# A smaller lead of the score maxima: 90 slots in place of 96 in a two-branch attention kernel

## The chip, the cores and the metric

The kernel runs on one NeuronCore of a Trainium2 chip. The metric is the device time of one execution in microseconds (us). The time before is 1738.96 us, the median of three runs (1738.92 to 1739.48). Engines are named as the profile names them: PE (TensorE matmuls) and PEld (its weight loads), DVE (VectorE), ACT (ScalarE), POOL (GpSimd), SP (SyncE, which here only starts transfers).

## What is computed

Two attention branches over the same 2048 x 512 input are mixed by a gate. A is softmax attention with 32 heads of 16 dimensions; B cuts the sequence into four segments of 512 rows, has causal softmax inside a segment, and adds a linear memory of the earlier segments.

```python
def reference(A_x, A_wqkv, A_wo, B_x, B_wq, B_wk, B_wv, B_wo, B_beta, gate_w):
    ...
        scores = jnp.einsum("bhqd,bhkd->bhqk", q, k) * scale
        p = _softmax(scores, axis=-1)
        o = jnp.einsum("bhqk,bhkd->bhqd", p, v)
    ...
        for s in range(N):
            logits = jnp.einsum("bhqd,bhkd->bhqk", qs, ks) * scale + mask
            p = _softmax(logits, axis=-1)
            a_dot = jnp.einsum("bhqk,bhkd->bhqd", p, vs)
            a_mem = num / den
            o = g * a_mem + (1.0 - g) * a_dot
    ...
    g = _sigmoid((x * gate_w).sum(-1, keepdims=True))
    return g * a + (1 - g) * b
```

## The kernel before

**Two stages.** The first stage makes queries, keys and values of both branches. It is cut into steps of 12 matmuls of 512 columns; work that goes beside them is posted on a step's number (`post_at`). From step S0 = 50 on come 32 steps for branch B's queries and keys, "segment tiles" (tile `pr`, line 385). Its memory is made beside them (tiles `tps`, `mps`, `num`, `den`).

The main stage runs over 2368 slots. A unit is four heads by one segment of 512 query rows: 32 units of A with 64 slots each (four heads by 16 blocks of 128 keys) and 32 of B with 10 slots. They alternate, an A unit and a B unit making 74 slots; at the end B comes before A. In a slot PE computes one score tile (tile `st`, line 1065; 50 rows of contraction: 48 of query and key and two that carry the row's maximum), and ACT takes its exponential into tile `p` (line 1088).

**The maxima.** A softmax row's maximum has to be known before its scores are made, since it enters the score product as two extra rows. So every score product is made once more, earlier, for its maximum alone: PE makes the product (tile `sm`, line 242), DVE reduces it (line 275 for A, line 290 with the causal mask for B). The list `maxs` holds all 2368 in the order in which they are made; slot n of the main stage makes the maximum of number n + LEAD. The first LEAD maxima are made in the first stage, in groups of four (`some_max`), beside the value pairs and beside some of the segment tiles. In a unit's 64 or 74 maxima the ten of a B unit stand at places that are multiples of three; `start` and `apart` say where, with special values for the unit numbers 1 and 31.

**From a maximum to its row.** After a unit's last maximum, POOL combines the partial maxima (`finish_max`). Then `transpose_max` turns them into rows on PE (tile `mt_ps`, line 232: one matmul per unit against the identity, into 32 rows of the bank), ACT copies them out (tile `mt`, line 235), and SP sends them into the query tile, behind which that unit's scores can start. `transpose_max` takes one or two units in one bank and with one copy. When it is called is set by a due number, counted in maxima: the end of the next A unit's maxima plus LATE_T = 9, but no later than `first[u] + LEAD - 12`, that is 12 slots ahead of the unit's first score. `run_late` looks at the end of every third slot and takes up to two units that are due. Where a call is made, no `fill` product is made in that step.

**Three slots at a time.** In the main stage PE makes the scores and maxima of three slots (a burst, in alternating row halves of the array), and then the value products that `most` allows (tile `ops`, line 155, with 17 columns of weights, in four strips of columns for four heads) or three products of other work from the list `shared` (in the same tile `ops`). Score tiles have three banks (`st`), maxima four (`sm`). The program's fp32 matmul shows as two in the trace.

**The end.** The last LEAD slots have no maximum to make. From slot `wide.start = nS - LEAD + 2` to `nS - 4` scores go into six banks, and steps are six slots long: up to 8 value pieces of 128 columns, and where these leave room, up to 11 less those of the products in `fill` (output products of an earlier block and the first closing products of the last one, into bank `sm`). What is left of the closing products is made behind the last value product.

Of the kernel before, what the change touches and what calls it, by code (L numbers as in the profile page):

```python
# [31 lines left out]

SLOTS = {"A": 64, "B": 10}
NU = 32
LEAD = 96
BURST = 3
LATER = (2, 3)
MOST = 3
# [9 lines left out]
def gated_mix(ctx, tc, x, xT, wqkv, a_wo, b_wq, b_wk, b_wv, b_wo, beta, gate_w, out):  # L48
# [52 lines left out]
    def unit(side, k):  # L101
        return side, k % NG, k // NG
# [15 lines left out]
    for k in range(NU):  # L118
        mine = {u: iter(range(32)) for u in range(2)}
        bs = [k - 1] if 0 < k < NU - 1 else [k - 1, k] if k else []  # L120
        theirs = {r: [(unit("B", b), (r, i)) for b in bs for i in range(5)] for r in range(2)}
        start, apart = (33, (3, 3)) if k == 1 else (6, (9, 3)) if k < NU - 1 else (23, (3, 3))
        at_ = [next(m for m in range(len(maxs) + start, len(maxs) + start + 6) if m % 3 == 0)]
        while len(at_) < 10 * len(bs):
            at_.append(at_[-1] + apart[len(at_) % 2])
        for m in range(len(maxs), len(maxs) + 64 + 10 * len(bs)):
            r = (m + 1) % 2
            if m in at_ and bs:
                maxs.append(theirs[r].pop(0))
            else:  # L130
                maxs.append((unit("A", k), (r, next(mine[r]))))
        assert not theirs[0] and not theirs[1]
    last_max = {u: m for m, (u, _) in enumerate(maxs)}
    a_last = sorted(last_max["A", k % NG, k // NG] for k in range(NU))
    first_max = {u: m for m, (u, _) in reversed(list(enumerate(maxs)))}
    assert len(maxs) == nS and all(first[u] + LEAD - last_max[u] > 24 for u in units)

# [19 lines left out]
    def wait_early(n):  # L157

        loads_ = []
        for m in range(n + 1 + LEAD, n + 1 + BURST + LEAD):  # L160
            if m < nS:
# [47 lines left out]
    def finish_max(u):  # L209
        nm = pmt.pop(u)  # L210
        if u[0] == "A":
            pm, nm = nm, mp.tile([128, 4, 4], F32, tag="nm", name="nm")
            dm = mp.tile([128, 4, 4, 2], F32, tag="dm", name="dm")
            nc.gpsimd.tensor_sub(dm, pm[:, :, :, 2:4], pm[:, :, :, 0:2])  # L214
            nc.gpsimd.tensor_scalar_min(dm, dm, 0.0)
            nc.gpsimd.tensor_add(dm, dm, pm[:, :, :, 0:2])
            nc.gpsimd.tensor_sub(nm, dm[:, :, :, 1], dm[:, :, :, 0])
            nc.gpsimd.tensor_scalar_min(nm, nm, 0.0)
            nc.gpsimd.tensor_add(nm, nm, dm[:, :, :, 0])

        ms = mp.tile([128, 2, 2, 2, 4], F32R, tag="ms", name="ms")
        nv = nm.rearrange("p (r h) s -> p r h s", r=2)
        nc.gpsimd.tensor_copy(ms[:, :, 0], nv)  # L223
        nc.gpsimd.tensor_sub(ms[:, :, 1], nv, ms[:, :, 0].bitcast(F32))
        return ms
# [37 lines left out]
    def max_part(m, bank, b=None):  # L263

        u, (r, i) = maxs[m]
        side, g, c = u
        if u not in pmt:
            pmt[u] = mp.tile([128, 4, 4] + [4] * (side == "A"), F32, tag="pm" + side, name="pm")
        pm = pmt[u]
        ps = bank()  # L270
        if side == "A":

            kc, s, h = i // 8, i % 8 // 2, 2 * r + i % 2
            max_product(ps, u, h, s, 0, CH, kt_[u, kc])
            nc.vector.tensor_reduce(pm[:, h, s, kc:kc + 1], ps, axis=AX.X, op=ALU.max, negate=True)  # L275
            was_read(b)
            flush_rows()
        else:


            k = kt_[u, c]
            if b is not None:
                read_last[b] = 9 * nS
            mine = [(2 * r + h, s, 128 * (s == 2) + 256 * (s == 1 and h), 128 * (s + 1))
                    for h, s in (((0, 0), (0, 2)), ((0, 1), (1, 1)), ((1, 0), (1, 2)), ((0, 3),), ((1, 3),))[i]]
            for h, s, n0, w in mine:
                max_product(ps, u, h, s, n0, w, k)
            flush_rows()
            def masked(h, s, n0, w):
                nc.vector.tensor_tensor_reduce(  # L290
                    out=tri["rest"][:, 0:w], in0=ps[:, n0:n0 + w], in1=tri["mask"][:, CH - w:], scale=-1.0, scalar=3.0e38,
                    op0=ALU.add, op1=ALU.min, accum_out=pm[:, h, s:s + 1])
                was_read(b)

            for h, s, n0, w in mine:
                rows_left.append(lambda h=h, s=s, n0=n0, w=w: masked(h, s, n0, w))
            rows_left.pop(0)()
        if m == last_max[u]:
            def finish():

                due = min(e for e in a_last if e >= last_max[u]) + LATE_T
                late.append((min(due, first[u] + LEAD - 12), u, finish_max(u)))
            todo.append((m + 1, finish))

    def run_todo(m):

        for e in [e for e in todo if e[0] <= m]:
            todo.remove(e)
            e[1]()

    def run_late(pool, tag, m):
        while us := [e for e in late if e[0] < m][:2]:
            for e in us:
                late.remove(e)
            transpose_max(us, pool, tag)
# [3 lines left out]
    def loads(m):  # L319

        m = min(m, len(maxs) - 1)
        while loaded[0] <= m:
            u, (r, i) = maxs[loaded[0]]
            if u not in qt:
                load_q(u)
            kc = u[2] if u[0] == "B" else i // 8
            if (u, kc) not in kt_:
                load_k(u, kc)
            loaded[0] += 1


    mnext = [0]
    with ExitStack() as p0:
# [61 lines left out]
        def post_at(n, place, f):  # L395
            posted.setdefault((n, place), []).append(f)
# [421 lines left out]
        def mem_q(c):  # L818

            banks = [me_sm.tile([128, CH], F32, tag="sm", name="num") for _ in range(4)]  # L820
            for o in range(NO):
                for i in range(4):
                    nc.tensor.matmul(banks[i][32 * o:32 * o + 32], mbd[o // 2][32 * i:32 * i + 32, o % 2].rearrange("p h e -> p (h e)"),  # L823
                                     pqs[o][32 * i:32 * i + 32], start=True, stop=True, tile_position=(32 * i, 32 * o))
            dps = me_ps.tile([128, CH], F32, tag="me", name="den")
            for o in range(NO):
                nc.tensor.matmul(dps[32 * o:32 * o + 32], zbd[:, o], pqs[o], start=True, stop=True,  # L827
                                 tile_position=(0, 32 * o))
            pqs.clear()

            ams = unit4(7, F32)

            def keep(i):
                nc.scalar.copy(ams[i], banks[i])  # L834
                nc.sync.dma_start(numd[c][i], ams[i])

            def keep_den():
                dn = wk1.tile([128, CH], F32, tag="dn", name="dn")
                nc.scalar.activation(dn, dps, AF.Identity, bias=eps)
                for o in range(NO):  # L840
                    nc.sync.dma_start(dend[c][8 * o:8 * o + 8], dn[32 * o:32 * o + 8])
            for i in range(4):
                keep(i)
            post(1, 2, keep_den)
# [35 lines left out]
        def some_max():  # L880
            m = mnext[0]
            if m == LEAD:
                return
            loads(m + 3 + PRE)
            for i in range(4):
                max_part(m + i, lambda: me_sm.tile([128, CH], F32, tag="sm", name="sm"))
            run_todo(m + 3)
            mnext[0] += 4
            run_late(me_ps, "me", mnext[0])

        post_at(36, 1, lambda: loads(16))
        for n in range(37, S0):
            post_at(n, 3, some_max)
# [6 lines left out]
        for n in range(32):  # L900
            if n in (14, 21, 29):
                post_at(S0 + n, 3, lambda c=n // 8: mem_q(c))
            elif n in (2, 4, 6, 8, 10, 12, 16, 18, 22, 24, 26):
                post_at(S0 + n, 3, some_max)

        def gates():
# [133 lines left out]

    wide = range(nS - LEAD + 2, nS - 4)
    assert wide.start % (2 * BURST) == wide.stop % (2 * BURST) == 0
# [115 lines left out]
    def octet(side, o, c, t0, vector=False):  # L1158
# [67 lines left out]
        if t0 is not None:  # L1226

            t0 += max([e + 2 - LEAD - t0 - ts[1] for e in a_last if 0 <= e + 1 - LEAD - t0 - ts[1] < 12], default=0)
        for n, f in zip(ts, (load, factors, send, factor, scale, store)):
# [117 lines left out]
    n = 0  # L1347
    while n < nS or queue or beside or filled[0] < len(fill):
# [4 lines left out]
        m = n + LEAD  # L1353
# [81 lines left out]
```

## Time and profile before

| | before |
|---|---|
| median of 3 runs | 1738.96 us |
| the profiled execution's own time | 1738.98 us |
| its span | 1737.1 us |
| first stage, up to the first score | 272.7 us |
| main stage with maxima (last DVE reduction ends) | to 1661.4 us |
| slots without maxima (last value product starts its end) | to 1715.2 us |
| closing products and the output | to 1737.1 us |

The span is the stretch between the first and the last instruction of the profiled execution; 1.9 us of its own time lie outside it. A row of a timeline gives the start in us, the time of the merged instructions, the engine, the line, the operation with tiles and shapes, and how many. Instructions on one engine can overlap in such rows, so the step from one row's start to the next one's tells more than a row's time. A row of the chain of waits gives start, time, engine and line of what released the next piece, followed back from the last instruction of the window.

### The profile page before, as it was taken

To read this page: it belongs to the slowest core of one execution; us is meant where nothing else is said; L and a number is where in the kernel's file an instruction comes from. 1 tells how busy PE (TensorE), PEld (TensorE's weight loads), DVE (VectorE), ACT (ScalarE), POOL (GpSimd) and SP (SyncE) were. 2 spreads that over 40 slices of the span, in tenths; PEclk is the share of its full clock that TensorE was granted. 3 is DMA by queue.
4 is the path that set the end of the run, shared out by engine and by line. 5 is a ranking of instruction groups with operands and counts; after the bars stand their busy time and mean duration, and the time that the engine had idled before them with its cause. 6 is when DMAs were issued, how large, how long until landed. Compare 5 with 4: busy or idle time off the path is not lost.

```text
span 1737.1 us, 41522 instructions
## 1 busy us (share of the span) xinstructions
PE 1729.1 (100%) x15157; PEld 875.5 (50%) x15157; DVE 1608.8 (93%) x3376; ACT 1439.9 (83%) x2774; POOL 706.8 (41%) x964
## 2 busy tenths in 40 slices
PE   9999999999999999999999999999999999999998
PEld 7877775444444444444444444444444444444444
DVE  7777987999999999999999999999999999999931
ACT  6543667888888888888888888888888888888884
POOL 1022544233353437444535353435354353435442
PEclk9999999999999999999999999999999999999999
DMA  7679887435453446454444453445444444444542
GB/s 246 193 241 238 303 278 218 112 93 156 116 159 102 142 124 175 132 141 125 137 138 143 133 148 122 134 140 139 141 123 149 131 141 113 144 119 147 149 152 63
DMA packets 168651, 264.97 MB, mean 153 GB/s; under 512 B 39512, under 2 KB 80760, under 8 KB 168448
## 3 DMA queue, kind: packets, MB, share of 16 engines
q1 hardware_dynamic: 166720, 260.78, 50.5%
q8 instruction: 121, 1.98, 0.5%
q0 software_dynamic: 1440, 1.14, 0.3%
q14 instruction: 82, 0.67, 0.1%
q10 hardware_dynamic: 288, 0.39, 0.1%
HBM read 177.74 MB, written 83.25 MB: 150 GB/s over the span
## 4 chain that ended last, share of the span: by engine, by line
PE 97%; DVE 1%; DMA 1%; ACT 0%; SPq 0%; issue 0%; ACTq 0%; DVEq 0%
PE ops L155 40%; PE st L1065 28%; PE sm L242 14%; PE pr L385 9%; PE pair L385 2%; PE sm L155 2%; DMA u<-xT 0%; PE mt_ps L232 0%; PE tps L851 0%; PE sm L1065 0%; DVE pm L275 0%; DMA u<-x 0%; PE mps L865 0%; PE num L823 0%; PE den L827 0%
## 5 line engine op out<-in xcount | busy, mean ns | idle before, releaser
L1088 ACT ACTIVATE p<-st 128x512 f32<-128x512 f32 x2261 | 1190.7, 600 | 146.8 <-PE sm L242 93.3
L275 DVE TENSOR_REDUCE pm<-sm 128x1 f32<-128x512 f32 x2048 | 1276.2, 682 | 8.3 <-PE sm L242 7.6
L242 PE MATMUL sm<-kA,qA 48*128 48x512 f32 x2048 | 662.2, 424 | 0.0
L1065 PE MATMUL st<-qA,kA 50*128 50x512 f32 x2014 | 655.9, 431 | 0.0
L155 PE MATMUL ops<-p,vA 128*17 128x256 f32 (+3 forms) x6360 | 552.2, 445 | 0.0
L1065 PEld LDWEIGHTS st<-qA,kA 50*128 50x128 f32 x2014 | 326.9, 185 | 423.4 <-ACT p L1088 379.7
L242 PEld LDWEIGHTS sm<-kA,qA 48*128 48x128 f32 x2048 | 337.8, 185 | 11.0 <-issue 4.2
L1189 POOL TENSOR_TENSOR rcp<-rec,minus 128x32 f32<-128x32 f32 x43 | 234.8, 5461 | 75.8 <-DMA rec<-dend 71.2
L290 DVE CUSTOM_DVE_ANT_0 rest<-sm,mask 128x128 f32<-128x128 f32 (+3 forms) x512 | 246.5, 481 | 0.0
L155 PEld LDWEIGHTS ops<-p,vA 128*17 128x17 f32 x6360 | 129.1, 96 | 215.7 <-issue 184.5
L1069 POOL TENSOR_SCALAR_AFFINE_SELECT p<-p 128x512 f32<-128x512 f32 x128 | 79.6, 638 | 267.6 <-ACT p L1088 263.1
L242 PE MATMUL sm<-kB,qB 48*128 48x128 f32 (+3 forms) x512 | 166.1, 384 | 0.0
L1065 PE MATMUL st<-qB,kB 50*128 50x512 f32 (+1 forms) x495 | 105.3, 329 | 0.3 <-ACT mt L235 0.3
L385 PE MATMUL pr<-u,u 128*128 128x512 f32 x392 | 101.4, 397 | 0.0
L1065 PEld LDWEIGHTS st<-qB,kB 50*128 50x128 f32 x495 | 68.5, 186 | 62.2 <-ACT p L1088 50.4
L155 PE MATMUL ops<-p,vB 128*17 128x128 f32 (+3 forms) x1504 | 88.3, 350 | 0.0
L385 PEld LDWEIGHTS pr<-u,u 128*128 128x128 f32 x392 | 71.8, 188 | 19.0 <-ACT u L834 2.5
L242 PEld LDWEIGHTS sm<-kB,qB 48*128 48x128 f32 x512 | 79.9, 184 | 0.0
L214 POOL TENSOR_TENSOR dm<-pm 128x32 f32<-128x32 f32 x32 | 7.8, 245 | 170.9 <-DVE pm L275 170.9
L434 POOL TENSOR_SCALAR mn<-full 128x512 f32<-128x512 f32 x24 | 39.0, 1625 | 53.8 <-ACT full L428 53.7
L223 POOL CAST ms<-pm 128x16 fp32r<-128x16 f32 x32 | 6.3, 198 | 127.5 <-DVE pm L290 127.5
L1205 POOL TENSOR_TENSOR v<-v,inv 128x512 f32<-128x512 f32 x31 | 39.8, 1284 | 28.7 <-DMA inv<-rdA 21.7
(227 smaller groups left out, 1422.5 us busy)
## 6 DMA issues: line engine op xcount, KB each, us to landing
kA<-kdA SPq DMA_DIRECT2D x256, 128.0 KB
vA<-vdA SPq DMA_DIRECT2D x31, 544.0 KB
kA<-kdA SPq DMA_DIRECT2D x256, 64.0 KB
kB<-kdB SPq DMA_DIRECT2D x192, 64.0 KB
qB<-qdB SPq DMA_DIRECT2D x192, 64.0 KB
kdA<-q SPq DMA_DIRECT2D x32, 256.0 KB
qA<-qdA SPq DMA_DIRECT2D x64, 128.0 KB
qdB<-q SPq DMA_DIRECT2D x32, 256.0 KB
```

The lines of the kernel that those rows point to most:

```text
L155: behind[0] = nc.tensor.matmul(*args, **kw)
L214: nc.gpsimd.tensor_sub(dm, pm[:, :, :, 2:4], pm[:, :, :, 0:2])
L242: nc.tensor.matmul(ps[:, n0:n0 + n], rows(qt[u][:, :, s * 128:(s + 1) * 128], h, 48), rows(k[:, :, k0:k0 + n], h, 48), start=True, stop=True)
L275: nc.vector.tensor_reduce(pm[:, h, s, kc:kc + 1], ps, axis=AX.X, op=ALU.max, negate=True)
L290: nc.vector.tensor_tensor_reduce(out=tri["rest"][:, 0:w], in0=ps[:, n0:n0 + w], in1=tri["mask"][:, CH - w:], scale=-1.0, scalar=3.0e38, op ...
L385: nc.tensor.matmul(ps, l, r, start=start, stop=stop, skip_group_check=chained)
L434: nc.gpsimd.tensor_scalar_min(ph["mn"], full, 0.0)
L1065: nc.tensor.matmul(ps[:, n0:n0 + CH - q0], rows(k[:, :, b * 128:(b + 1) * 128], h, 50), rows(q[:, :, q0:], h, 50), start=True, stop=True)
L1069: nc.gpsimd.affine_select(out=x, in_=x, pattern=[[0, 4], [1, 128]], base=0, channel_multiplier=-1, compare_op=ALU.is_ge, fill=0.0)
L1088: nc.scalar.activation(p[:, h], ps, AF.Exp, scale=SCALE)
L1189: eng.tensor_tensor(r, rec, minus, op=ALU.pow)
L1205: eng.tensor_mul(k["v"], k["v"], k["inv"])
```

## The change

LEAD goes from 96 to 90. The six maxima move from the first stage to the main stage. In the segment tiles one group of four goes (groups at S0 + 10 and S0 + 12 become one at S0 + 11), and the last group, at S0 + 26, makes two. The places of the B maxima among the maxima of units 1 and 31 are put six numbers earlier. `wide.start` is worked out from LEAD, so the end without maxima is six slots shorter.

```diff
-LEAD = 96
+LEAD = 90
...
-        start, apart = (33, (3, 3)) if k == 1 else (6, (9, 3)) if k < NU - 1 else (23, (3, 3))
+        start, apart = (27, (3, 3)) if k == 1 else (6, (9, 3)) if k < NU - 1 else (17, (3, 3))
...
-            for i in range(4):
+            for i in range(min(4, LEAD - m)):
                 max_part(m + i, lambda: me_sm.tile([128, CH], F32, tag="sm", name="sm"))
-            run_todo(m + 3)
-            mnext[0] += 4
+            run_todo(min(m + 3, LEAD - 1))
+            mnext[0] = min(m + 4, LEAD)
...
-            elif n in (2, 4, 6, 8, 10, 12, 16, 18, 22, 24, 26):
+            elif n in (2, 4, 6, 8, 11, 16, 18, 22, 24, 26):
                 post_at(S0 + n, 3, some_max)
```

On PE in the first stage, behind the step S0 + 12, the group of maxima goes and so does the transposition of the first unit's rows (`+` and `-` as in the program of the change against that of before; `u` are operands of the segment tiles):

```order
 L385 MATMUL pr<-u_1810,u_1640 128x512
 L385 MATMUL pr<-u_1809,u_1640 128x512
-L242 MATMUL sm<-kA_196,qA_1644 128x512 x4
-L232 MATMUL mt_ps<-identf,ms 32x128
 L385 MATMUL pr<-u_1809,u_1641 128x512
 L385 MATMUL pr<-u_1810,u_1640 128x512
```

The steps S0 + 12 and S0 + 13 now follow each other without a break; the group stands behind S0 + 11, ahead of `mps`, and the transposition behind the group of S0 + 16.

On PE in the main stage, at the end of the first A unit's scores, before:

```order
L1065 MATMUL st<-qA_1644,kA_199 128x512
L242 MATMUL sm_3248<-kA_196,qA_4093 128x512
L155 MATMUL ops<-p,vA 17x128 x4
L155 MATMUL ops<-p,vA 17x256 x4
L232 MATMUL mt_ps<-identf,ms 32x128 x2
L1065 MATMUL st<-qA_1644,kA_199 128x512
L242 MATMUL sm_3245<-kB_200,qB_4158 128x128
```

And now, in the same place:

```order
L155 MATMUL ops<-p,vA 17x256 x8
L232 MATMUL mt_ps<-identf,ms 32x128
L1065 MATMUL st<-qA_1644,kA_199 128x512
L242 MATMUL sm_3230<-kB_200,qB_4192 128x128
L242 MATMUL sm_3230<-kB_200,qB_4192 128x384
L1065 MATMUL st<-qA_1644,kA_199 128x512
L242 MATMUL sm_3227<-kA_196,qA_4126 128x512
L1065 MATMUL st<-qA_1644,kA_199 128x512
L242 MATMUL sm_3228<-kA_196,qA_4126 128x512
L155 MATMUL ops<-p,vA 17x256 x4
L155 MATMUL ops<-p,vA 17x128 x4
L232 MATMUL mt_ps<-identf,ms 32x128
```

A B unit and an A unit were transposed in one call. Their due numbers fall apart now: B's is `first[u] + LEAD - 12`, which came down by six, A's is nine behind the end of its maxima, which didn't. In the whole program the calls go from 33 (31 with two units) to 64 with one each, and ACT's copies (line 235) with them; 30 of the 31 calls that are added stand in the main stage with maxima, one behind it.

On PE at the end, the last closing products ahead of the last score and the first behind the last values, before:

```order
L155 MATMUL sm_3246<-wB,qclosed 128x512 x3
L155 MATMUL sm_3247<-wB,qclosed 128x512
L1065 MATMUL st<-qA_22283,kA_199 128x512
L155 MATMUL ops<-p,vA 17x512 x8
L155 MATMUL sm_3247<-wB,qclosed 128x512 x2
L155 MATMUL sm_3248<-wB,qclosed 128x512 x3
```

And now:

```order
L155 MATMUL sm_3227<-wB,kA_194 128x512 x3
L155 MATMUL sm_3227<-wA,kA_195 128x512
L1065 MATMUL st<-qA_22403,kA_199 128x512
L155 MATMUL ops<-p,vA 17x512 x8
L155 MATMUL sm_3227<-wA,kA_195 128x512 x2
L155 MATMUL sm_3228<-wB,qclosed 128x512 x3
```

The list `fill` is six products further behind: 56 in place of 50 closing products stand between the last values and the last two pairs of blocks (`hl`).

## The prediction

> **What bounds the kernel now.** I read the totals of the page first, then the chain of waits and the busy times of the main stage alone, then timelines of single bursts. All sums are made against the profiled execution's own 1738.98 us (its span of 1737.1 and 1.9 around it), which is 0.02 us above the median of the runs, 1738.96.
>
> ```profile
> PE 1729.1 (100%) x15157; PEld 875.5 (50%) x15157; DVE 1608.8 (93%) x3376; ACT 1439.9 (83%) x2774; POOL 706.8 (41%) x964
> ```
>
> PE's 100% says little, since the ends of matmuls are modelled. Two answers for the main stage say more: the busy times from 280 to 1655 us (PE, weight loads, DVE, ACT, POOL), and the chain of waits over the same stretch.
>
> ```profile
> 280.00:1655.00 1375.00, 1375.00 (x12921) 627.90 (x12921) 1374.34 (x2949) 1225.62 (x2372) 595.71 (x816) 1.00 0.47 135
> by line: PE ops L155 49.1%; PE st L1065 34.2%; PE sm L242 16.2%; PE mt_ps L232 0.4%; issue 0.0%
> ```
>
> DVE is busy for 1374.34 of 1375 us, so it is nearly full. Yet the chain runs through PE alone: not one step of it is a DVE, ACT or DMA step. Both are loaded to the brim, and the chain says whose delay counts. Two DVE rows, each an unbroken run of reductions of A maxima, tell which of the two waits (the page's row for these reductions stands ahead of them):
>
> ```profile
> L275 DVE TENSOR_REDUCE pm<-sm 128x1 f32<-128x512 f32 x2048 | 1276.2, 682 | 8.3 <-PE sm L242 7.6
> ...
> 381.29 13.83 DVE L275 TENSOR_REDUCE pm<-sm 128x1 f32<-128x512 f32 x23
> 562.45 8.81 DVE L275 TENSOR_REDUCE pm<-sm 128x1 f32<-128x512 f32 x14
> ```
>
> One reduction takes 0.68 us by itself, and they overlap. From start to start it is (13.83 - 0.68) / 22 = 0.598 us in the first run, DVE's own pace, and (8.81 - 0.68) / 13 = 0.625 in the second, slower, in gaps too short to be listed as idle time. In the second stretch DVE waits for PE, in the first it doesn't. So PE sets the pace in part of the time and DVE is just behind it in the rest; there is next to no cover for new work on PE.
>
> **Six maxima leave the first stage.** The chain there, in the segment tiles, with what follows each group:
>
> ```profile
> 193.26 0.66 PE sm L242 x4
> 193.92 0.59 PE tps L851 x4
> 194.51 2.73 PE pr L385 x12
> 197.24 0.70 PE mps L865 x59
> 197.94 2.94 PE pr L385 x12
> 200.88 0.66 PE sm L242 x4
> 201.54 0.34 PE mt_ps L232 x2
> 201.88 5.68 PE pr L385 x24
> ...
> 254.66 0.67 PE sm L242 x4
> ```
>
> All of it is PE work on the chain. The group at 193.26 goes: -0.66. It comes back ahead of `mps` at 197.24: +0.66. The group at 200.88 goes with its transposition, and so does the break in the stream of products (12 products take 2.94 ahead of a break that stands alone, 2.73 without): -0.66 - 0.34 - 0.21 = -1.21. The transposition comes back later: +0.34. The last group, at 254.66, makes two of four: -0.3, about half. Sum **-1.2 us**. DVE has six reductions fewer in this stage and is not on this part of the chain. Bounds: -0.5, if a transfer or DVE takes over somewhere, and -3.6, six reductions at 0.598, if DVE did set the pace.
>
> **Six slots of the main stage get a maximum.** DVE's full pace prices them at 6 x 0.598 = **+3.6 us**; two bursts of three slots. Value pieces and scores of these six slots come along, and they are counted off the end below. Bounds: +3.3, two of the shorter bursts (1.66 us from 390.84 to 392.50 below), and +3.75 at the slower 0.625.
>
> **The transposition is taken apart.** This is the term that decides. The order shows 30 more calls in the main stage, each with a matmul on PE, a bank of `st`, an ACT copy and its transfers; the matmuls and the transfers are no more than before, the calls are. What does a call cost PE? The bursts at 391 and at 395 us each have three value pieces ahead of the next score:
>
> ```profile
> 390.84 0.50 PE L1065 MATMUL st<-qA,kA 50*128 50x512 f32 x1
> ...
> 391.73 0.84 PE L155 MATMUL ops<-p,vA 128*17 128x384 f32 x8
> 392.50 0.50 PE L1065 MATMUL st<-qA,kA 50*128 50x512 f32 x1
> ...
> 393.43 1.06 PE L155 MATMUL ops<-p,vA 128*17 128x128 f32 x16
> ...
> 395.38 0.84 PE L155 MATMUL ops<-p,vA 128*17 128x128 f32 x16
> 396.05 0.39 PE L232 MATMUL mt_ps<-identf,ms 128*32 128x128 f32 x4
> 396.36 0.50 PE L1065 MATMUL st<-qA,kA 50*128 50x512 f32 x1
> ...
> 1660.86 0.85 PE L155 MATMUL ops<-p,vA 128*17 128x256 f32 x16
> 1661.53 0.38 PE L232 MATMUL mt_ps<-identf,ms 128*32 128x128 f32 x2
> 1661.84 0.91 PE L1065 MATMUL st<-qA,kA 50*128 50x512 f32 x3
> ```
>
> From the first value product to the next score it is 0.77 us without a call, 0.98 with a call of two units and again 0.98 with a call of one unit (x2 in the trace). So a call costs 0.21 us, whatever its units; the second unit was free, beside the first. The chain of the main stage agrees: 0.4% of 1375 us for 30 calls is 0.18 us each. Taken in full, 30 x 0.21 = 6.3 us.
>
> What could hide it is PE's waiting. There is little:
>
> ```profile
> 504.49 0.50 PE L1065 MATMUL st<-qA,kA 50*128 50x512 f32 x1
> ...
> 505.53 0.84 PE L155 MATMUL ops<-p,vB 128*17 128x128 f32 x16
> ```
>
> The score and maximum part of this burst takes 1.04 us, where others take 0.93 (392.50 to 393.43) or 0.89 (390.84 to 391.73). Such a burst stands once in two of three units, some 20 times in all, and makes about 20 x 0.13 = 2.6 us in which PE was ahead of DVE. I let half of that, 1.3 us, absorb added PE work, since a delay elsewhere in the unit isn't given back there. Term: **+5.0 us**. Bounds: 0, if DVE's pace hides it all, and 30 x 0.39 = 11.7, if the matmul's whole time in its row counted. I stay near the 0.21 that the step from row to row gives twice. ACT's copies, one more a unit, lie in ACT's free time: it is busy for 1225.62 of 1375 us.
>
> **The end.** Before, the first six slots without maxima ran from 1661.84 to the row at 1665.84: 4.00 us, because eight `fill` products stood in them. These slots are gone from the end.
>
> ```profile
> 1665.84 0.73 PE L1065 MATMUL st<-qA,kA 50*128 50x512 f32 x3
> ...
> 1668.78 0.50 PE L1065 MATMUL st<-qB,kB 50*128 50x512 f32 x2
> ...
> 1673.11 0.73 PE L1065 MATMUL st<-qB,kB 50*128 50x256 f32 x5
> ...
> 1694.66 0.72 PE L1065 MATMUL st<-qA,kA 50*128 50x512 f32 x3
> ...
> 1697.60 0.72 PE L1065 MATMUL st<-qA,kA 50*128 50x512 f32 x3
> ...
> 1715.18 1.42 PE L155 MATMUL sm<-wB,qclosed 128*128 128x512 f32 x5
> ...
> 1726.94 2.92 PE L155 MATMUL sm<-wB,hl 128*128 128x512 f32 x12
> 1729.70 2.88 PE L155 MATMUL sm<-wA,hl 128*128 128x512 f32 x12
> ```
>
> But `fill` is not less. In the steps that are left, by the order, the first two (before: 2.94 us up to 1668.78 and 4.33 from there to 1673.11, where a score had to wait for ACT's copy and seven `fill` products stood) now have four value pieces and one call each, and no `fill` product. Without `fill` a step is as long as 1694.66 to 1697.60, 2.94 us; with a call's 0.21 some 3.2, so 6.4 in place of 7.27: -0.9. The next steps with `fill` have 11, 9, 9 and 7 products where there were 9, 6, 6 and 6: nine more. A closing product takes (1726.94 - 1715.18) / 50 = 0.235 us: +2.1. And six more stand behind the last values: +1.4. That piece is PE's alone:
>
> ```profile
> 1727.59 0.42 DVE L1214 TENSOR_TENSOR hl<-v,hl 128x256 fp32r<-128x256 f32 x1
> ```
>
> The last block's operand is ready at 1728.01, and PE comes to it at 1729.70, so 1.7 us of PE work would have to go before anything else became late there. The end: -4.0 - 0.9 + 2.1 + 1.4 = **-1.4 us**. Bounds: -3.5, if the nine products that stand earlier find PE free, and 0, if a row's transfer is waited for in the two short steps and they gain nothing.
>
> **The sum.** -1.2 + 3.6 + 5.0 - 1.4 = +6.0: 1738.98 + 6.0 = **1745.0 us**, 0.35% slower.
>
> **The rivals.** (1) *The calls are hidden.* If DVE sets the pace, PE's 0.21 us lie in its waits and the sum is -1.2 + 3.6 - 1.4 = +1.0: 1740.0. For it speaks DVE's 1374.34 of 1375 us; against it that no DVE step is in the chain, and 0.625 us a reduction in the second DVE row. By the Trainium skill (Perfetto Trace Analysis, Identifying the Most-Contended Engine) the busy time of matmuls is no measure of how loaded TensorE is, the busy share of its weight loads is, and VectorE's occupancy is a fair measure; by that rule PE would be loaded to 46% (627.90 of 1375) and VectorE would be the bound, which gives this rival's time; the chain of this trace speaks against it. Chance 0.18.
>
> (2) *Faster: the B maxima come to stand better.* Relative to the scores they move six slots. In a burst with a B maximum DVE is the slower one, in bursts with four value pieces PE is; where the two coincide more often, DVE's short waits go. The second DVE row loses 13 x 0.027 = 0.4 us; if each third unit has such a stretch, that is 10 x 0.4 = 4 us. Together with hidden calls: +1.0 - 4.0 = -3.0, 1736.0. It decides only if the reductions come to 0.598 us in every run. The 30 calls load PE, which this needs to be relieved; chance 0.04.
>
> (3) *The rows come late.* A unit's rows are sent six slots nearer to its scores. Before:
>
> ```profile
> 398.25 1.27 SPq L238 DMA_DIRECT2D qA<-mt x2
> ...
> 409.16 0.50 PE L1065 MATMUL st<-qA,kA 50*128 50x512 f32 x1
> ```
>
> The issue ends at 399.52, the A unit's first score (behind ten slots of B) starts at 409.16: 9.6 us; six slots less leave 6. If the SP queue is held for longer than that in each unit, PE waits perhaps 1 us 30 times: 1770. Nothing in the profile shows such a hold; chance 0.03.
>
> That the change doesn't do what it says is excluded by the order, which shows the six maxima in their new places.
>
> **How the numbers follow.** My forecast (the calls cost PE most of 0.21 us each) has a chance of 0.75, with 1742 to 1748 as its own range. The range is to hold 8 in 10: it takes in the forecast's range but for its upper edge, and most of the hidden case, **1739.5 to 1747.5**. 0.2% is 3.5 us, about what a measurement of this kernel can tell from no change: slower than 1742.4 is nearly all of the forecast and the late rows, 0.73; within it are the hidden calls, the forecast's low edge and most of the better places of B, 0.24; faster 0.03.
>
> **What would show it.** Right: 64 calls of `mt_ps`, each some 0.2 us in the chain of waits, its share from 0.4% to about 0.8% in the main stage; the stretch from the first to the last reduction of the main stage longer by more than 8 us (3.6 for the maxima, 5 for the calls), with DVE's mean per reduction up. Also a first score about 1.2 us earlier, and about 1.4 us more between the last value product and the `hl` products. Wrong: a main stage longer by 3.6 us alone (rival 1); bursts of scores that wait for a transfer (rival 3); or a first stage that saves more than 2 us, which would mean that DVE set the pace there.

## The result, and the profile after

The changed kernel takes 1756.01 us (median of four runs, 1753.37 to 1759.05) beside 1738.94 us for the kernel before (median of four): a ratio of 1.0103, with an interval of 1.009 to 1.0115. That is 17.1 us slower, where 6.0 were forecast; the direction was right, the size was not. The profiled execution of the changed kernel took 1756.53 us, with a span of 1754.8.

The page of the changed kernel, busy times and the chain of waits by engine:

```profile
PE 1738.5 (99%) x15157; PEld 881.7 (50%) x15157; DVE 1612.7 (92%) x3376; ACT 1445.3 (82%) x2805; POOL 707.2 (40%) x964
...
PE 95%; DMA 2%; DVE 1%; ACT 1%; issue 0%; POOL 0%; SPq 0%; DVEq 0%; ACTq 0%
```

The same two views as before for the main stage of the changed kernel, 280 to 1655 us: busy times, and the chain of waits by line.

```profile
280.00:1655.00 1375.00, 1371.31 (x12832) 629.49 (x12831) 1366.21 (x2915) 1221.52 (x2385) 587.14 (x807) 1.00 0.49 134
by line: PE ops L155 48.2%; PE st L1065 33.2%; PE sm L242 16.3%; PE mt_ps L232 0.8%; DMA qB<-mt 0.4%; DMA kA<-kdA 0.3%; ACT p L1088 0.2%; POOL p L1069 0.1%; issue 0.1%; POOL v L1205 0.1%; POOL v L1207 0.1%; ACT part L1279 0.0%; SPq L238 0.0
```

Two things are new. `mt_ps` has doubled to 0.8%, as forecast. And the chain, which was PE alone before, now has transfers in it: rows of maxima (`qB<-mt`) and keys (`kA<-kdA`). DVE's idle time in this window went from 0.66 to 8.79 us (1375 less its busy time): it waited along with PE.

**Where the 17.7 us of span lie.** ACT makes one exp for each of the 2368 slots, so the starts of the exps, counted from the first, give the time of every slot in both traces. Here "both early" is an experiment told below.

| stretch | forecast | changed kernel | both early |
|---|---|---|---|
| start-up, to the 49th product of `pr` and `pair` | 0 | +2.1 | -0.3 |
| from there to the first exp | -1.2 | -1.3 | -1.5 |
| slots 0 to 2274 (30 calls more) | +5.0 | **+11.4** | +5.7 |
| slots 2274 to 2280 (six maxima more, no `fill`) | -0.4 | -0.4 | -0.3 |
| slot 2280 to the last exp | +1.2 | **+5.0** | +2.9 |
| the rest | +1.4 | +0.9 | -0.5 |
| sum | +6.0 | +17.7 | +6.1 |

The first row is no effect of the change: its code is the same. In the timeline of PE, the first product behind the value pair's eviction starts at 18.15 us before (first fence) and at 20.24 in this execution of the changed kernel (second):

```profile
18.15 0.50 PE L385 MATMUL pr<-kA,qtmp 128*128 128x512 f32 x1 [0.84 <-DVE vs L550]
```

```profile
20.24 0.50 PE L385 MATMUL pr<-kA,qtmp 128*128 128x512 f32 x1 [1.81 <-DVE vs L550]
```

In the profiles of the twelve runs told below it starts at 17.5 to 18.6 us. The exps themselves, by form, with the first and the last start behind the durations, before and after:

```profile
L1088 ACT ACTIVATE p<-st x2261: 588/598/680, 273.9 to 1713.4; 128x512 f32<-128x512 f32 x189
```

```profile
L1088 ACT ACTIVATE p<-st x2264: 588/599/682, 274.7 to 1730.3; 128x512 f32<-128x512 f32 x189
```

The first exp is 0.8 us later and not 1.2 earlier; less the 2.1 of start-up that is a gain of 1.3.

**The main stage, first cause: the calls.** A stretch without any stall shows their price. This is the view by windows, ACT's work on `p` alone; 1111 exps are 1110 slots, 15 times 74. Before:

```profile
771.18:1448.48 677.30, 583.42 (x1111) 1.00 0.46 134
```

The same slots of the changed kernel:

```profile
778.22:1458.18 679.96, 584.00 (x1111) 1.00 0.48 134
```

2.66 us more in 15 pairs of units, with one call more in each: 0.18 us a call if the calls are all of it, 5.3 us for 30. This term of the forecast was right in size. The stretch holds the shift of six slots too: in `pair_soon`, a run told below that has the shift without these calls, it takes 678.24 us, so about 1.7 of the 2.66 us are shown to be the calls'.

**Second cause: operands that come late.** The remaining 6 us of the main stage stand in a few places. Over twelve slots at a time, the slots fall behind those of the kernel before by 1.7 and 1.2 us between 478 and 498 us, by 2.4 near 676, 1.1 near 1587 and 1.4 near 1631; some of it is made up elsewhere. PE's timeline near 676 us in the changed kernel (idle time ahead of a row, and what ended it, in brackets):

```profile
670.67 0.84 PE L155 MATMUL ops<-p,vA 128*17 128x128 f32 x16
671.33 0.38 PE L232 MATMUL mt_ps<-identf,ms 128*32 128x128 f32 x2
671.64 0.50 PE L1065 MATMUL st<-qA,kA 50*128 50x512 f32 x1
...
679.35 0.38 PE L155 MATMUL ops<-p,vA 128*17 128x128 f32 x2 [1.82 <-DMA qB<-mt]
```

The call of one unit is there, 0.97 us from value product to score as forecast. But PE then stands still. The last value product of a burst carries the wait for all landings that the next three slots need (`wait_early`); here it waits for B's rows, transposed at 671.33 and copied out by ACT by 672.01. What SP did in that time:

```profile
670.96 0.58 SPq L1255 DMA_DIRECT2D blk<-hdA  x1
671.59 0.47 SPq L1255 DMA_DIRECT2D blk<-hdB  x1
672.10 0.47 SPq L1018 DMA_DIRECT2D vA<-vdA  x1
672.67 2.64 SPq L177 DMA_DIRECT2D kA<-kdA  x4
675.41 1.41 SPq L238 DMA_DIRECT2D qB<-mt  x2
```

The rows (line 238) come up only at 675.41, 3.4 us after they were ready, behind loads of the output's steps, of values and of keys. The second place is earlier, at 484.77 us, where PE waits 0.87 us for keys:

```profile
484.77 0.81 PE L155 MATMUL ops<-p,vA 128*17 128x384 f32 x2 [0.87 <-DMA kA<-kdA]
```

SP there, in the changed kernel:

```profile
472.52 0.47 SPq L1198 DMA_DIRECT2D rdA<-rec  x1
476.19 0.55 SPq L1202 DMA_DIRECT2D inv<-rdA  x1
476.80 1.96 SPq L177 DMA_DIRECT2D qA<-qdA  x4
479.18 1.69 SPq L177 DMA_DIRECT2D kA<-kdA  x4
```

SP stood from 472.99 to 476.19, because `inv` reads what the store ahead of it writes. By the Trainium skill (DMA: Bandwidth & Descriptors, Anatomy of one DMA) a transfer's wait for a semaphore is spent on the engine that issues it, before it is handed on; the trace agrees, with 3.2 us in which SP issued nothing. The loads of `qA` and `kA` stood behind it. In the kernel before they went ahead of the same pair:

```profile
464.85 1.95 SPq L177 DMA_DIRECT2D qA<-qdA  x4
466.90 1.75 SPq L177 DMA_DIRECT2D kA<-kdA  x4
...
469.24 0.40 SPq L1198 DMA_DIRECT2D rdA<-rec  x1
474.65 0.55 SPq L1202 DMA_DIRECT2D inv<-rdA  x1
```

So the change moved more than maxima. Loads of queries and keys are issued PRE = 20 numbers ahead of the maxima, and the maxima are six slots nearer to the scores; the output's steps hang on the value products, which did not move. On SP's queue, loads and rows slid six slots back between steps that wait.

**The end.** PE's waits in the last steps of the changed kernel:

```profile
1674.07 0.49 PE L1065 MATMUL st<-qA,kA 50*128 50x512 f32 x1
...
1677.64 0.77 PE L1065 MATMUL st<-qA,kA 50*128 50x512 f32 x3
...
1681.36 0.45 PE L1065 MATMUL st<-qB,kB 50*128 50x384 f32 x1 [1.06 <-ACT mt L235]
...
1684.39 0.59 PE L155 MATMUL ops<-p,vA 128*17 128x512 f32 x1 [1.25 <-DMA qB<-mt]
...
1693.38 0.38 PE L155 MATMUL ops<-p,vB 128*17 128x128 f32 x2 [1.25 <-DMA qA<-mt]
```

Two bursts of three slots with maxima take 3.57 us, as forecast (+3.6). Then the rows of the last two units, now in calls of their own and six slots apart, are waited for at three places: the copy first, then B's rows, then A's. A fourth wait of the end, 0.78 us for DVE's `res` (line 1283) at 1704.01 us, isn't in the kernel before either. It comes in all twelve runs below and was not followed up.

### The profile page after: what moved, and what is told of

Same layout as the page of the kernel before. It is cut to its first block, busy times and chain, and to the rows that moved or that the text cites. A ratio compares the mean times of both kernels' runs of the same rounds, so it can differ in the third digit from the quotient of the medians.

```text
span 1754.8 us, 41627 instructions
## 1 busy us (share of the span) xinstructions
PE 1738.5 (99%) x15157; PEld 881.7 (50%) x15157; DVE 1612.7 (92%) x3376; ACT 1445.3 (82%) x2805; POOL 707.2 (40%) x964
## 4 chain that ended last, share of the span: by engine, by line
PE 95%; DMA 2%; DVE 1%; ACT 1%; issue 0%; POOL 0%; SPq 0%; DVEq 0%; ACTq 0%
PE ops L155 40%; PE st L1065 27%; PE sm L242 14%; PE pr L385 9%; PE pair L385 2%; PE sm L155 1%; PE mt_ps L232 1%; DMA u<-xT 1%; DMA qB<-mt 0%; DMA qdB<-q 0%; ACT p L1088 0%; PE tps L851 0%; DMA qA<-mt 0%; DVE pm L275 0%; PE sm L1065 0%
## 5 line engine op out<-in xcount | busy, mean ns | idle before, releaser
L275 DVE TENSOR_REDUCE pm<-sm 128x1 f32<-128x512 f32 x2048 | 1279.7, 691 | 12.9 <-PE sm L242 11.5
L242 PEld LDWEIGHTS sm<-kA,qA 48*128 48x128 f32 x2048 | 335.5, 185 | 10.5 <-issue 4.6
L1069 POOL TENSOR_SCALAR_AFFINE_SELECT p<-p 128x512 f32<-128x512 f32 x128 | 79.8, 640 | 223.4 <-ACT p L1088 218.5
```

Source lines behind the costliest of these rows:

```text
L242: nc.tensor.matmul(ps[:, n0:n0 + n], rows(qt[u][:, :, s * 128:(s + 1) * 128], h, 48), rows(k[:, :, k0:k0 + n], h, 48), start=True, stop=True)
L1069: nc.gpsimd.affine_select(out=x, in_=x, pattern=[[0, 4], [1, 128]], base=0, channel_multiplier=-1, compare_op=ALU.is_ge, fill=0.0)
```

## The experiments

Theory 1: operands come late, because loads and rows have slid on SP's queue. Theory 2: it is the calls, which are dear. Each run has its own runs of the kernel before on the same chip; the us given as a difference are between those two medians. On this scale the changed kernel stands at +17.1.

One thing has to be read with these times, the TensorE clock that was granted. In the traces of the kernel before, of the changed kernel, of `split_only` and of `both_early` it is 1.00 from 8 us on to the last 2.1 us, so the table above compares like with like. In the other traces it falls to 0.50 for a while, during a wait of PE or soon behind it. With the last 4 us of each trace left out it is at 0.50 for 3.4 us in all in `brows_early`, `mid26`, `end_rows` and `pair_soon`, 6.8 in `rows_act`, 10.2 in `factor_later`, 13.7 in `paired`, 20.5 in `lead102`, 23.9 in `pre26` and 105.9 in `rows_pool`. There a late operand can cost more than the wait that the timeline shows; `lead102` below is an example.

### The calls taken back, or added alone

`paired`:

```diff
-                late.append((min(due, first[u] + LEAD - 12), u, finish_max(u)))
+                late.append((min(due, first[u] + LEAD - (6 if first[u] < nS - 100 else 12)), u, finish_max(u)))
```

> The changed kernel, but with the bound on a B unit's rows at LEAD-6 (the last two units keep LEAD-12), so that one call transposes two units again: 34 calls in place of 64, and B's rows are sent some four slots later. Theory 1 (operands come late): a call costs only the 0.16 us by which each pair of units is longer in the changed kernel (45.04 against 44.89 us for 74 slots), so 30 calls less give 4.8 us, and the places where PE waits for landings of qB, qA and kA stay or grow: 1751 us, or more if the later B rows add waits. Theory 2 (the calls are what is dear, with what they hold up on SP's queue): nearly all of the 17 us goes, 1741 to 1743.

Measured: 1775.39 us beside 1737.21, +38.2, ratio 1.0222 (1.0208 to 1.0236). Theory 2 is out: with the 30 calls gone the kernel is 21 us slower still. Theory 1 had said "or more". Part of it is the clock, 0.50 for 6.8 us from 685.25 on at the first of these two places in PE's timeline:

```profile
687.67 0.59 PE L155 MATMUL ops<-p,vA 128*17 128x128 f32 x2 [6.18 <-DMA qB<-mt]
...
1103.38 0.38 PE L155 MATMUL ops<-p,vA 128*17 128x128 f32 x2 [1.22 <-DMA qB<-mt]
```

The second kind comes back in every third pair of units, since a call is looked for at every third slot only. B's rows, some four slots later, miss their burst even where SP is free. So in the changed kernel the calls of one unit are not the loss: with LEAD 90 they buy rows that come in time.

`split_only`, on the kernel before:

```diff
-                late.append((min(due, first[u] + LEAD - 12), u, finish_max(u)))
+                late.append((min(due, first[u] + LEAD - 18), u, finish_max(u)))
```

> The kernel before, LEAD 96, with only the bound at LEAD-18: B's rows leave four slots sooner in calls of their own (64 calls), all maxima, loads and rows else where they were. Theory 1 (operands come late because of the six slots): only the price of 30 calls, 30 x 0.16 = 4.8 us, and no matmul that waits for a landing: 1743 to 1745. Theory 2 (the calls are dear): 1750 to 1756, with PE waiting for qB or qA as in the changed kernel.

Measured: 1746.18 beside 1737.21, +9.0, ratio 1.0053 (1.004 to 1.0065). The chain of its main stage holds nothing that is late:

```profile
by line: PE ops L155 48.8%; PE st L1065 33.7%; PE sm L242 16.5%; PE mt_ps L232 0.9%; ACT p L1088 0.1%; ACT part L1279 0.0%; issue 0.0%
```

The 1110 slots in its middle:

```profile
774.11:1454.93 680.82, 583.39 (x1111) 1.00 0.46 133
```

3.52 us more than before, 0.23 a call, 7.0 for 30. Both theories missed: the run is 3 to 5 us over theory 1's +4 to +6, and has none of theory 2's late operands. The last 1.8 us lie behind slot 2274 and were not followed up.

### Rows sooner, loads sooner

`brows_early`: the same bound, LEAD - 18, in the changed kernel.

> The changed kernel (LEAD 90) with the bound at LEAD-18: B's rows leave six slots sooner, the calls stay 64. Theory 1: the waits for qB (about 2.4 us at 676, 1.4 at 1631, 0.7 each at 496 and 1587, and at the end about 1.8 for B's last unit) go, the wait for kA at 482 us stays: about 1750. Theory 2 (the calls are dear wherever they stand): 1756.

Measured: 1751.44 beside 1737.21, +14.2, ratio 1.0084 (1.007 to 1.0097), some 3 us less than the changed kernel where 6 were expected. The waits at 1587 and 1631 us are gone, those at 482, 496 and 676 stay. At 676 the rows are issued sooner, at 672.79, but PE still waits 1.5 us for their landing; what the longer burst at 496 us waits for the profile doesn't name.

`pre26`:

```diff
-PRE = 20
+PRE = 26
```

> The changed kernel with loads of q and k 26 maxima ahead in place of 20, which puts them back to the slots they had beside scores, values and the output's steps in the kernel before. Theory 1, first half (loads of q and k have slid behind steps of the output on SP's queue): the wait for kA at 482 us goes, 1.7 to 2.4 us, and some of the waits for qB behind loads of kA or qB (676, 1631): 1750 to 1754. Theory 1, other half (only the rows are late): 1754 to 1756. Theory 2 (the calls are dear): 1756.

Measured: 1769.95 beside 1737.21, +32.7, ratio 1.0191 (1.0177 to 1.0205). A miss as a whole, and yet slots 0 to 2146 are without a stall: 4.5 us over the kernel before, the price of the calls. The loss lies around them: the first exp comes at 280.9 us, 7 us later, and the slots from 2146 to 2274 take 14 us more. In the first stage PE waits 1.8 us, up to 240.27, and the granted clock is 0.50 for 3.4 us from 240.55; the rest of the 7 us was not followed up. In the later slots PE waits 6.45 us for `kB`, up to 1643.54, and the granted clock is 0.50 from 1640.0 to 1660.5. So I put the loads forward in the middle alone.

`mid26`:

```diff
-            loads(m + PRE)
+            loads(m + PRE + 6 * (n < nS - 250))
```

> The changed kernel with loads of q and k 26 maxima ahead in slots 0 to 2117 alone, 20 in the first stage and in the last 250 slots. Theory 1 in its first half (the six slots put the loads behind steps of the output on SP's queue, and the loads stand ahead of the rows): the jumps at 482 to 498 us (2.4), 676 (2.4), and those near 1587 and 1631 (2.0) go, about 7 us: 1749. Rows late by themselves: the waits for qB at 676 and 1631 us stay, only some 3 us go: 1753. Neither: 1756.

Measured: 1749.02 beside 1739.29, +9.7, ratio 1.0053 (1.0039 to 1.0067): 7.4 us less, as the first half of theory 1 has it. No key is waited for in the main stage any more, and of the waits for rows a single one is left, at 673 us.

`end_rows`:

```diff
-                late.append((min(due, first[u] + LEAD - 12), u, finish_max(u)))
+                late.append((min(due, first[u] + LEAD - 12) - 6 * (first[u] > nS - 80), u, finish_max(u)))
```

> The changed kernel with the rows of the last two units one group of six slots sooner. If the end is longer because these rows come late (PE waits there for ACT's copy of the transposed rows, for qB and for qA, 0.8 + 1.75 + 1.75 us beyond the usual step): 3.5 to 4.3 us less, about 1752. If it is longer because closing products that had found PE free now stand in its way: no change, 1756.

Measured: 1753.32 beside 1739.29, +14.0, ratio 1.0083 (1.0069 to 1.0097): 3.1 us less, just short of the 3.5 to 4.3 expected. The waits for `qB` and `qA` at the end are gone, the one for ACT's copy is not. The edit does a second thing: with the calls in other steps, `fill` products find room again, and 50 closing products stand behind the last values, as in the kernel before, in place of the changed kernel's 56. Behind the last exp's start this trace is 1.35 us shorter than the changed kernel's. So the run doesn't part what late rows cost from what these six products cost.

`both_early`, the last two diffs together:

> The changed kernel with both: loads 26 ahead in slots 0 to 2117, and the last two units' rows one group sooner. All six slots are moved and all 64 calls are there, but no operand should be late. If late operands are all that the forecast lacked, its four terms (-1.2 +3.6 +5.0 -1.4) are left: 1745, give or take 1.5. If one of the four terms is wrong as well, 1748 or more.

Measured: 1744.93 us (1743.33 to 1746.09) beside 1739.29, +5.6, ratio 1.0032 (1.002 to 1.0045). All six maxima are moved, all 64 calls are made, and 11.5 of the 17.1 us are gone. The chain of its main stage has no transfer left:

```profile
by line: PE ops L155 48.8%; PE st L1065 33.9%; PE sm L242 16.2%; PE mt_ps L232 0.9%; ACT p L1088 0.2%; issue 0.1%; ACT part L1279 0.0%
```

Two waits are left at its end. One is for ACT's copy of the rows, where the next score needs the bank, the other for `res`:

```profile
1673.22 0.44 PE L1065 MATMUL st<-qB,kB 50*128 50x384 f32 x1 [0.83 <-ACT mt L235]
...
1687.54 0.96 PE L155 MATMUL sm<-wB,qclosed 128*128 128x512 f32 x3 [0.78 <-DVE res L1283]
```

What is left adds up to the forecast's sum, +6.1 in the trace beside +6.0. Up to slot 2280 it does so row by row in the table above, within 0.7 us. At the end only the total agrees: +2.9 and -0.5 where +1.2 and +1.4 were forecast, since here too 50 closing products stand behind the last values and not 56.

### What holds SP

`factor_later`, the changed kernel with the load of `inv` issued later:

```diff
-        ts = ... else (0, 10, 25, 29, 42, 54)
+        ts = ... else (0, 10, 25, 34, 42, 54)
```

> The changed kernel with one load of the output's steps (inv, the reciprocals broadcast) issued nine slots behind the store that it reads, in place of four. SP stood 3.2 us at this load at 473 to 476 us, and the loads of qA and kA that PE waits for at 484.77 us stood behind it. If it is such holds that make the loads late: the wait at 484.77 goes, and the jump near 482 to 498 us shrinks by 1.5 to 2.4 us: 1753.5 to 1754.5, and the jump at 676 us, where no such hold stood, stays. If the loads are late for another reason (their own issue, or the transfers' time): 1756.

Measured: 1756.71 beside 1738.78, +17.9, ratio 1.0098 (1.0084 to 1.0112): no gain in the median. Its trace shows both halves. SP now has the loads of `qA` at 471.61 us, ahead of `inv`, and no wait of PE stands near 482. But near 676 us the wait has grown from 1.82 to 2.59 us:

```profile
677.20 0.38 PE L155 MATMUL ops<-p,vA 128*17 128x128 f32 x2 [2.59 <-DMA qB<-mt]
```

Behind it the granted clock is 0.50 for 3.4 us, and for 6.8 us more at the end, from 1681.98 on, which it isn't in the changed kernel's trace. The hold as the cause of the wait at 482 us is shown by this. What the repair is worth is open: three of its four runs had a mean granted clock of 0.997 and took 1756.7 to 1756.8 us, the fourth, at 1.000, took 1752.2.

`rows_pool`, the changed kernel with `nc.gpsimd.dma_start` for the rows in line 238:

> The changed kernel with the transfers of the rows (qB and qA from mt) issued by POOL in place of SP; all times and orders else as in the changed kernel. If the rows are late because they stand behind loads and stores on SP's queue (at 676 us kA's loads, vA and blk stood ahead of them from 671.3 to 675.4): the waits for qB and qA at 496, 676, 1587, 1631, 1684 and 1693 us shrink or go, the one for kA at 482 stays: 1750 to 1752. If the rows are late because the transposition itself stands too near to the scores, or because POOL's own queue (one of its steps takes 5.46 us) holds them as long: 1756 or more.

Measured: 1872.72 beside 1737.97, +134.8, ratio 1.0779 (1.0764 to 1.0794). POOL's timeline:

```profile
696.01 5.46 POOL L1189 TENSOR_TENSOR rcp<-rec,minus 128x32 f32<-128x32 f32 x1
...
703.62 1.24 POOL L238 DMA_DIRECT2D qB<-mt  x2 [0.37 <-issue]
```

The rows stand behind the output's power step and its followers, longer than on SP. This is the other case that was expected, at a much larger size: PE waits 79.8 us for B's rows at 15 places, and at each of them the granted clock falls to 0.50, for 105.9 us in all.

`rows_act`, the same with `nc.scalar.dma_start`:

> The changed kernel with the transfers of the rows issued by ACT, right behind its own copy of the transposed rows, so that nothing of the loads, stores or POOL's steps stands ahead of them. If the rows are late because they stand behind other transfers on SP's queue: the waits for qB and qA at 496, 676, 1587, 1631 us and at the end shrink by the time that they stood there, the wait for kA at 482 us stays, and ACT's issues (1.27 us for the two of a unit on SP) find room beside its exps (busy for 82% of the span): 1750 to 1752. If the issues hold up the exps that PE's scores wait for: up to 0.5 us each, 64 x 0.5 = 32 us more, 1780.

Measured: 1842.58 beside 1737.78, +104.8, ratio 1.0605 (1.0591 to 1.062). ACT's timeline at one call:

```profile
688.14 0.25 ACT L235 CAST mt<-mt_ps 32x128 fp32r<-32x128 f32 x1
688.42 1.28 ACTq L238 DMA_DIRECT2D qB<-mt  x2
689.75 1.58 ACT L1088 ACTIVATE p<-st 128x512 f32<-128x512 f32 x3 [1.36 <-PE st L1065]
```

The 1.36 us in brackets are ACT's own two issues (its next score had long been made, at 688.37 to 688.67 us), and PE's later scores wait for ACT. If each of the 64 calls costs as much as this one, that is 87 of the 105 us, an estimate. So these two runs say nothing on SP's queue; they say that a held issue costs what its engine is worth.

### Two more sums

`pair_soon`, `both_early` with the calls paired again:

```diff
-LATE_T = 9
+LATE_T = 6
...
-                late.append((min(due, first[u] + LEAD - 12) - 6 * (first[u] > nS - 80), u, finish_max(u)))
+                late.append((min(due + 3, first[u] + LEAD - 12) - 6 if first[u] > nS - 80 else min(due, first[u] + LEAD - 6), u, finish_max(u)))
```

> The run both_early (six slots moved, loads 26 ahead, the last two units' rows a group sooner) with the 30 calls taken back: a unit A's rows leave three slots sooner (LATE_T 6) and B's bound is LEAD-6, so that both go in one call, 34 in all, some three slots before the place where B's rows go alone in the changed kernel's groups. If 30 calls cost about 5 us, as the forecast has it, what is left is -1.2 +3.6 -1.4 = +1.0: 1740, five less than both_early, with 74 slots at 44.9 us again. If the longer 74 slots (45.0 against 44.9 us) come from the six slots' shift itself: 1744 to 1745, no change from both_early. If three slots are too few for POOL and DVE to have the rows ready: PE waits for ms or for ACT's copy, over 1745.

Measured: 1751.03 beside 1738.78, +12.3, ratio 1.0077 (1.0063 to 1.009). The 1110 slots in the middle, of this run and then of `both_early`:

```profile
774.06:1452.30 678.24, 583.39 (x1111) 1.00 0.47 134
```

```profile
770.82:1450.83 680.01, 583.54 (x1111) 1.00 0.46 134
```

There 15 calls are worth 1.77 us, 0.12 each and 3.5 for 30. But the whole is 6.7 us slower than `both_early` and not 5 faster, since rows are late again, at the end (1.52 us ahead of a score at 1673.07, with the granted clock at 0.50 for 3.4 us behind it) and above all here:

```profile
675.54 0.38 PE L155 MATMUL ops<-p,vA 128*17 128x128 f32 x2 [3.19 <-DMA qB<-mt]
```

`lead102`, the change the other way (six more maxima in the first stage, 33 calls):

```diff
-LEAD = 90
+LEAD = 102
...
-        start, apart = (27, (3, 3)) if k == 1 else (6, (9, 3)) if k < NU - 1 else (17, (3, 3))
+        start, apart = (39, (3, 3)) if k == 1 else (6, (9, 3)) if k < NU - 1 else (23, (3, 3))
...
-            elif n in (2, 4, 6, 8, 11, 16, 18, 22, 24, 26):
+            elif n in (2, 4, 6, 8, 10, 12, 16, 18, 20, 22, 24, 26, 28):
```

> The other way: LEAD 102, six more maxima in the first stage, the bound at LEAD-12 as it is, which leaves 33 calls. By the terms of the forecast with the sign turned: +1.2 -3.6 +1.4 = -1.0, within 0.2% of the kernel before. If any shift of six slots breaks the fit of loads and the output's steps on SP's queue: +4 or more, with PE waiting for kA or qB. If rows come sooner and nothing else: up to -2.

Measured: 1761.39 beside 1739.29, +22.1, ratio 1.0128 (1.0114 to 1.0142). The terms with the sign turned do not hold either; six slots the other way break the fit too. The slots from 2146 to 2274 alone take 13 us more. SP there:

```profile
1627.33 1.92 SPq L177 DMA_DIRECT2D kA<-kdA  x4
1633.58 0.34 SPq L1127 DMA_DIRECT2D odA<-oraw  x1
1634.28 2.67 SPq L174 DMA_DIRECT2D qB<-qdB  x6
1637.06 2.69 SPq L174 DMA_DIRECT2D kB<-kdB  x6
```

The last B unit's loads stand behind the store of an A unit's value sums, for which SP stood 4.3 us (from 1629.25), and PE waits for them:

```profile
1640.27 0.66 PE L1065 MATMUL st<-qB,kB 50*128 50x384 f32 x1 [6.66 <-DMA kB<-kdB]
```

The wait is only half of the 13 us. The granted clock, third from the end of a row of the view by windows, is 0.50 from 1635.47 to 1655.95 us:

```profile
1640.00:1650.00 10.00, 9.73 (x33) 6.28 (x35) 4.86 (x14) 3.97 (x8) 1.81 (x3) 0.50 0.29 81
1650.00:1660.00 10.00, 10.00 (x80) 4.57 (x78) 7.66 (x17) 7.41 (x15) 6.89 (x3) 0.70 0.07 26
```

If work takes twice as long at half the clock, the 15.7 us from 1640.27 on hold a loss of 7.8, an estimate; with the wait that is 14.5, a little over the 12.9 us measured.

No version here beats the kernel before; the nearest is `both_early`, 0.3% slower.

## Why the forecast was right in direction and wrong in size

- **What bounds the kernel**: right. PE's chain set the time: in `both_early`, where no transfer is left in the main stage's chain, the work added to PE comes to +5.6 us, of +6.0 forecast.
- **The first stage, -1.2**: -1.3 and -1.5 in the two profiles of the table, but such a small term isn't settled by them. Six other profiles of kernels with the same first stage (`paired`, `brows_early`, `mid26`, `end_rows`, `pair_soon`, `factor_later`) have -1.8 to -0.2, and `split_only`, with the first stage of before, has +0.5. In the changed kernel's profile 2.1 us of start-up, which the code does not explain, lie on top of it.
- **Six slots with maxima, +3.6 less 4.0 of the end's first slots**: right, 3.57 us beside 4.00.
- **The calls taken apart, +5.0**: right in size. By pairs of kernels a call costs 0.12 to 0.23 us, 3.5 to 7.0 us for 30, and in the changed kernel itself 5.3 if the calls are all of the 2.66 us above. Rival 1, the hidden calls, is out. But "the matmuls and the transfers are no more than before" passed over that the calls were taken apart *because* the rows had come nearer to their scores: `paired`, with the calls joined at B's later place, is 21 us slower than the changed kernel, and `pair_soon`, with the calls joined sooner, 6.7 us slower than `both_early`.
- **The end, -1.4**: mis-sized. It measured +1.9 in the changed kernel (-4.0 +5.0 +0.9) and -1.6 in `both_early` (-4.0 +2.9 -0.5), where no row's transfer is waited for and six closing products stand ahead of the last values again. I had given late rows there the bound "0, if a row's transfer is waited for in the two short steps and they gain nothing"; a wait can cost more than the gain, and there are three. That the last A unit's call now comes six slots later was not priced.
- **Rival 3, the rows come late**: the step that failed. The sum put waits for transfers at nothing. In the changed kernel's profile they and what followed them cost 6.1 us in the main stage (11.4 less 5.3 for the calls), and the end is 3.8 us over its forecast behind slot 2280 (5.0 less 1.2), 0.8 of it the wait for `res`. I wrote "Nothing in the profile shows such a hold" and gave it 0.03. The profile of before does show holds. SP's own waits in it, in the view of waits (in all, times, the longest, us):

```profile
SPq L1127 <- ACT oraw L1126: 244.2, 56, 10.5
SPq L238 <- ACT mt L235: 81.2, 15, 8.5
...
SPq L1202 <- DMA rdA<-rec: 25.4, 11, 4.9
```

SP stands up to 10.5 us at a single store, and my 9.6 us of spare were less six slots only 6. I had read one unit's rows, at 398.25 us, where SP happened to be free. Nor did I price the second thing that moved, the loads of queries and keys, though the forecast's sum needs SP's order of them to stay; put back in the middle of the main stage, they give 7.4 us (`mid26`). The rival's shape was wrong too: not 1 us in each of 30 units, but 0.7 to 2.4 us in a few places of the main stage, and three waits at the end.
- **The signs named ahead**: 64 calls at 0.8% of the chain, seen; 1.4 us more between the last value product and the `hl` products, 1.37 seen (12.28 us before, from 1714.66 to 1726.94, and 13.65 now); a main stage longer by more than 8 us, seen, 15.0 from the first exp to the last reduction's start, of which the forecast explains 8.6; a first score 1.2 us earlier, not seen in this profile; "bursts of scores that wait for a transfer", named as the sign of rival 3, seen. Rival 2 (faster) did not come.

## What to carry to other kernels

When work is moved by some slots, list every queue that it is moved past, with its waits, ahead of any sum: the view of waits for SP's queue shows how long a transfer behind it may stand, and a spare read in one place is no bound for the others. A part of a change that looks like overhead may be what pays for the rest; take it out alone before it is blamed. And when a forecast is low by a clean amount, remove the suspected extra and see whether the sum comes back: here it did, to +5.6 of +6.0. Then see whether it comes back term by term; at the end it did not.

## What was not expected of the hardware

- An issue on ACT is not free beside its work: two cost 1.28 us of ACT's time, 1.36 us between exps, and the kernel with all 128 of them on ACT is 105 us slower.
- POOL's power step on 128x32 elements takes 5.46 us, and the rows issued by POOL stood behind it.
- The first 20 us of the same code differ by up to 2.7 us between profiles (17.5 to 20.2 us to the same product), as much as some effects looked for here.
- A wait of PE can cost more than its length. In `lead102` the granted clock fell to 0.50 during a wait of 6.66 us and stayed there for 20.5 us; in `rows_pool` it did so at 15 waits of 4.1 to 7.3 us, for 6.8 or 10.2 us each. In the changed kernel's profile, with waits up to 1.82 us, it stayed at 1.00.
